# First batch loaded into output tiles, its last tokens for several pairs at once, and feed-forward products moved among the last key tiles

## The chip, the cores and the metric

The kernel runs on one core of one Trainium2 chip. The core has TensorE (PE in the profile, PEld for its weight loads), VectorE (DVE), ScalarE (ACT), GpSimd (POOL) and SyncE (SP), each with a list of its own that it works off in order, and 16 DMA engines. SP and ACT issue transfers on hardware queues (q1, q10), POOL on the software queue (q0), which also converts types. The metric is the device time of one execution in microseconds; lower is better.

## The reference

```python
def _attn_ref(q, k, v, tau):
    q_n = q / (np.linalg.norm(q, axis=-1, keepdims=True) + 1e-06)
    k_n = k / (np.linalg.norm(k, axis=-1, keepdims=True) + 1e-06)
    scores = np.matmul(q_n, k_n.transpose(0, 1, 3, 2)) / tau
    scores = scores - np.max(scores, axis=-1, keepdims=True)
    attn = np.exp(scores)
    attn = attn / (np.sum(attn, axis=-1, keepdims=True) + 1e-09)
    return np.matmul(attn, v)
# x = attention output, (batch, heads, seq, dim) -> (batch * seq, heads * dim)
h = x @ w_in
out = np.maximum(0.01 * h, h) @ w_out
```

q, k and v are (8, 12, 448, 64) in 32-bit floats, tau is 0.1, x is 3584 x 768, w_in 768 x 2048 and w_out 2048 x 768. So: attention on normalised queries and keys, then two dense layers with a leaky ReLU between them.

## The kernel before

**Pairs.** Work on attention goes by pairs of heads, six to a batch, numbered 0 to 47 (called s). A pair's q and k, 448 tokens each, come in three parts: 384 main tokens of q, 384 of k (each token row of 64 numbers, three rows in line to a partition), and the last 64 tokens of both, q's on partitions 0 to 63 and k's on 64 to 127 of one slot. `load_qk` (L126) issues four transfers for a pair: two for the main tokens (192 KB each), two for the last tokens (32 KB each). They go into one of four buffers (`ldp`, L50), and so pair s + 4 can be asked for only when pair s has been normalised.

**Steps of a pair.** `squares` (L193, POOL, for the first pairs also ACT and DVE) squares q and k; `sums` (L208, DVE) adds up the 64 squares of each row, in two parts: q with the last tokens, and k; `roots` (L224, ACT) takes the root as an exponential of half a logarithm; `normalise` (L232, DVE) adds the small constant, inverts, and multiplies into bf16; `transposes` (L281) turns the result on PE and copies it from the accumulator memory with DVE (`qkT`). Then `scores` (L315) multiplies keys by queries in key tiles of 128 tokens on PE, and ACT takes the exponential (L338). Key tile 3 holds the last 64 keys of two pairs, so odd pairs have four tiles and even ones three.

**Quads.** Two pairs make a quad (four heads, called j). `totals` (L356) adds up the exponentials with products with ones and inverts them on ACT; `products` (L366) multiplies by v, once for each half e of the dimensions; `scale` (L375, DVE) multiplies by the inverse into `xT` (L340), the transposed attention output in bf16, one tile for two batches, two buffers (`xtp`, L60). Row block kt = 2 j + e of `xT` belongs to quad j and half e.

**Feed-forward.** Batch c is a chunk of 384 or 512 tokens. `first` (L466) makes one of 16 row blocks of the hidden layer from six products over kt (one accumulator bank), and ACT evicts it through the leaky ReLU (L483); `second` (L489) multiplies by w_out and DVE copies the result (L516). `first` could be split in two parts, kt below a limit and the rest. w_in is loaded in four transfers by POOL (`load_w_in`, L103): even kt and odd kt of the first half of its columns, then of the second half.

**Order.** The whole order is written out by hand up to pair 12; after that a planner spreads feed-forward work over the visits of key tiles. Before the loop over the six pairs of batch 0 (L621 to L677), pair 0 and most of pair 1 are prepared (L548 to L617). The loop runs scores of pair s beside the preparation of pairs s + 1 to s + 3. `fill` (L573) multiplies a constant tile: 22 products ahead of everything, then two or three at the places where it is called. Behind the loop (L688 to L747) feed-forward products of chunk 0 run among the key tiles of batch 1. `hold` (L583) is a copy of one column on POOL, which makes POOL's list wait for a tile before it issues further loads. Accumulator banks are dealt by `banks` (L76): the oldest free one, or a pair of them for a key tile; a bank can be kept under a name.

**Waiting of transfers.** SP's and ACT's transfers use eight completion counters in turn, so a transfer is issued only when the eighth before it has landed. POOL's transfers have eight of their own.

Of the kernel before, what the change touches and what calls it, by code (L numbers as in the profile page):

```python
# [16 lines left out]
def kernel(  # L17
# [108 lines left out]
    def load_qk(s, engs=(nc.sync, nc.sync), rem_engs=None):  # L126
        if s >= NSLOT:
            return
        whole = ldp.tile([128, 14 * D], F32, name="qk_h")
        if s >= OLD:  # L130
            u, which = divmod(s - OLD, 2)
            for w, pair in enumerate(UNITS[u][1]):
                b, h0 = pair // NPAIR, 2 * (pair % NPAIR)
                nc.sync.dma_start(
                    out=whole[64 * w : 64 * w + 64],
                    in_=(q, k)[which][b, h0 : h0 + 2].rearrange("h (p t) d -> (h p) (t d)", t=14),
                )
            raw[s] = whole
            return
        b, h0 = s // NPAIR, 2 * (s % NPAIR)  # L140
        q_h, k_h = halves(whole)
        engs[0].dma_start(out=q_h[:, :, 0:3], in_=main(q, b, h0, 2))
        engs[1].dma_start(out=k_h, in_=main(k, b, h0, 2))
        for i, (x, eng) in enumerate(zip((q, k), rem_engs or engs)):
            eng.dma_start(
                out=q_h[64 * i : 64 * i + 64, :, 3],
                in_=x[b, h0 : h0 + 2, MAIN:S].rearrange("h p d -> p h d"),
            )
        raw[s] = (q_h, k_h)
# [318 lines left out]
    def first(c, m, lo=0, hi=KT):  # L468
        c0, n = chunk_cols(c)
        if c not in hT:  # L470
            hT[c] = htp.tile([128, MT, 512], BF16, name="hT")
        pm = begun.pop((c, m)) if lo else banks(1)
        for kt in range(lo, hi):
            nc.tensor.matmul(  # L474
                out=pm[:, :n],
                lhsT=w_in_sb[:, kt, m * 128 : (m + 1) * 128],
                rhs=xT[c // 2][:, kt, c0 : c0 + n],
                start=(kt == 0), stop=(kt == KT - 1),
            )
        if hi < KT:  # L480
            begun[c, m] = pm
            return
        nc.scalar.activation(out=hT[c][:, m, :n], in_=pm[:, :n], func=AF.Prelu, alpha=0.01)  # L483
# [63 lines left out]

    load_qk(0, (nc.sync, nc.scalar))  # L548
    load_qk(1, (nc.sync, nc.scalar), (nc.sync, nc.sync))
    load_qk(2)  # L550
    load_qk(3)
# [69 lines left out]
    for s in range(NPAIR):  # L621
# [3 lines left out]
        last = s == NPAIR - 1  # L625
        if s == 1:
            roots(2)
        scores(s, (0,))
# [6 lines left out]
        if not last:  # L635
            normalise(s + 1)
            load_qk(s + 5)
# [4 lines left out]
        if last:  # L642
            load_w_out(0)
# [3 lines left out]
        if s == 0:  # L647
            sums(2)
            load_v_rem(0, range(2, 4))
# [5 lines left out]
        elif s != 1:  # L655
            load_w_in(max(s - 1, 0))
# [3 lines left out]
        if not even or s == 0:  # L660
# [15 lines left out]
        if j is not None and not even:  # L676
# [14 lines left out]
    scale(late.pop(), 1)  # L691
    totals(j)
    sums(s)
# [15 lines left out]
    sums(s + 1)  # L709
    feed_groups(0, 1)  # L710
    transposes(s)
    roots(s + 1)
    feed_groups(0, 1)
# [3 lines left out]
    feed_groups(0, 1)  # L717
    scores(s, (0, 1, 2))
    feed_groups(0, 1)
# [218 lines left out]
```

## Time and profile before

| | |
|---|---|
| median of three runs | 421.89 us (420.99 to 422.38) |
| profiled execution, its own time | 421.03 us |
| its span, first to last instruction | 419.2 us |
| PE, ACT, DVE, POOL busy | 98%, 61%, 53%, 28% |
| filler products on PE up to 60 us | 15.59 us, 53 products |
| DMA, mean over the span | 128 GB/s; 207 GB/s in the first 60 us |

In the profile's rows "L329" is a line of the kernel before. A row of the timeline gives the start in microseconds from the span's start, the length, the engine, the line, the operation, the tile written and the tile read, the shapes, how many instructions were merged, and in brackets how long the engine had stood idle and what ended that. A row of the windows gives a stretch, its length, and the busy time and count of each engine. Matmuls overlap, so a busy PE is not PE at its peak; what matters is whether its list has gaps.

### The profile page before, as it was taken

To read this page: it belongs to the slowest core of one execution; us is meant where nothing else is said; L and a number is where in the kernel's file an instruction comes from. 1 tells how busy PE (TensorE), PEld (TensorE's weight loads), DVE (VectorE), ACT (ScalarE), POOL (GpSimd) and SP (SyncE) were. 2 spreads that over 40 slices of the span, in tenths; PEclk is the share of its full clock that TensorE was granted. 3 is DMA by queue.
4 is the path that set the end of the run, shared out by engine and by line. 5 is a ranking of instruction groups with operands and counts; after the bars stand their busy time and mean duration, and the time that the engine had idled before them with its cause. 6 is when DMAs were issued, how large, how long until landed. Compare 5 with 4: busy or idle time off the path is not lost.

```text
span 419.2 us, 11328 instructions
## 1 busy us (share of the span) xinstructions
PE 410.0 (98%) x4797; PEld 211.9 (51%) x4797; DVE 223.0 (53%) x385; ACT 254.4 (61%) x430; POOL 116.6 (28%) x149
## 2 busy tenths in 40 slices
PE   7899999999999999999999999999999999999996
PEld 2334555544455555544455555554445555654563
DVE  6886886874687555864583864464621311210021
ACT  4896877377766686757874778547764364014300
POOL 3877472431433223512430523131210000000000
PEclk9999999999999999999999999999999999999999
DMA  6999999485387932884275592743441100010021
GB/s 164 173 232 231 221 236 225 107 238 113 84 196 224 215 79 57 203 205 115 60 181 160 126 233 74 170 121 89 90 89 52 66 38 3 38 77 0 2 75 75
DMA packets 41906, 53.82 MB, mean 128 GB/s; under 512 B 12544, under 2 KB 32256, under 8 KB 41856
## 3 DMA queue, kind: packets, MB, share of 16 engines
q1 hardware_dynamic: 25680, 40.88, 34.9%
q0 software_dynamic: 15488, 11.80, 19.8%
q8 instruction: 37, 0.61, 0.6%
q10 hardware_dynamic: 688, 0.43, 0.4%
q14 instruction: 13, 0.11, 0.1%
HBM read 45.61 MB, written 11.01 MB: 135 GB/s over the span
## 4 chain that ended last, share of the span: by engine, by line
PE 89%; DMA 3%; DVE 3%; ACT 3%; issue 0%; SPq 0%; DVEq 0%
PE ps L505 35%; PE ps L474 33%; PE ps L425 9%; PE ps L400 7%; PE ps L349 3%; DMA qk_h<-in_q_dram 3%; DVE qn L253 2%; ACT pe L338 1%; PE ps L329 1%; PE ps L576 1%; DMA qk_h<-in_k_dram 1%; PE ps L267 1%; ACT ss L227 0%; ACT hT L483 0%; ACT norms L228 0%
## 5 line engine op out<-in xcount | busy, mean ns | idle before, releaser
L505 PE MATMUL ps<-w_out_sb,hT 128*128 128x384 bf16 x896 | 151.3, 326 | 0.4 <-DVE xT L380 0.4
L474 PE MATMUL ps<-xT,w_in_sb 128*128 128x384 bf16 (+1 forms) x768 | 150.8, 353 | 0.0
L406 ACT ACTIVATE pe<-ps 128x896 bf16<-128x896 f32 x126 | 108.9, 915 | 44.6 <-PE ps L400 44.6
L505 PEld LDWEIGHTS <-hT 128*128 128x128 bf16 x896 | 85.5, 98 | 65.2 <-issue 10.3
L474 PEld LDWEIGHTS <-w_in_sb 128*128 128x128 bf16 x768 | 72.8, 98 | 74.0 <-issue 9.2
L483 ACT ACTIVATE hT<-ps 128x384 bf16<-128x384 f32 (+1 forms) x128 | 67.6, 550 | 54.1 <-PE ps L474 53.6
L516 DVE COPY osb<-ps 128x384 f32<-128x384 f32 (+1 forms) x56 | 30.8, 551 | 101.3 <-PE ps L505 100.3
L199 POOL TENSOR_TENSOR sq<-qk_h 128x896 f32<-128x896 f32 x36 | 60.5, 1681 | 3.3 <-DMA qk_h<-in_k_dram 3.2
L585 POOL CAST seen<-qn 128x1 f32<-128x1 bf16 x46 | 8.9, 193 | 173.7 <-DVE qn L243 168.0
L243 DVE TENSOR_TENSOR qn<-qk_h,r 128x896 bf16<-128x896 f32 x36 | 42.5, 1182 | 1.4 <-DVE r L237 0.2
L338 ACT ACTIVATE pe<-ps 128x896 bf16<-128x896 f32 x42 | 35.9, 915 | 2.4 <-PE ps L329 2.3
L214 DVE TENSOR_REDUCE ss<-sq 128x14 f32<-128x896 f32 x36 | 37.3, 1037 | 0.0
L400 PE MATMUL ps<-qkT 64*32 64x448 bf16 x1008 | 36.5, 353 | 0.0
L236 DVE TENSOR_REDUCE r<-norms 128x14 f32<-128x28 f32 x48 | 8.6, 179 | 49.2 <-ACT norms L228 48.7
L227 ACT ACTIVATE ss<-ss,tiny 128x14 f32<-128x14 f32 x48 | 14.7, 306 | 28.5 <-DVE ss L214 25.6
L450 DVE TENSOR_TENSOR xT<-ps,rb 128x448 bf16<-128x448 f32 x32 | 18.4, 617 | 22.3 <-PE ps L425 21.2
L289 DVE STREAM_TRANSPOSE tt<-qn 128x448 f32<-128x448 f32 x36 | 29.6, 821 | 0.9
L425 PE MATMUL ps<-pe,vq 64*32 64x448 bf16 x1008 | 27.0, 349 | 0.0
L206 POOL TENSOR_TENSOR sq<-qk_h 128x384 f32<-128x384 f32 (+1 forms) x21 | 20.8, 1009 | 14.9 <-DMA qk_h<-in_k_dram 14.9
L400 PEld LDWEIGHTS <-qkT 64*32 64x32 bf16 x1008 | 13.2, 91 | 19.3 <-issue 14.5
L425 PEld LDWEIGHTS <-vq 64*32 64x32 bf16 x1008 | 14.5, 93 | 8.0 <-issue 0.3
L253 DVE TENSOR_TENSOR qn<-qk_h,r 128x512 bf16<-128x512 f32 (+1 forms) x24 | 18.2, 798 | 0.4
(52 smaller groups left out, 215.8 us busy)
## 6 DMA issues: line engine op xcount, KB each, us to landing
qk_h<-in_q_dram SPq DMA_DIRECT2D x36, 224.0 KB, 4.3
qk_h<-in_k_dram SPq DMA_DIRECT2D x36, 224.0 KB, 4.4
out_dram<-osb SPq DMA_DIRECT2D x20, 384.0 KB, 3.0
qkT<-tt SPq DMA_DIRECT2D x72, 56.0 KB, 3.3
qkT<-tt SPq DMA_DIRECT2D x36, 112.0 KB, 3.5
vq<-in_v_dram POOLq DMA_DIRECT2D x16, 224.0 KB, 5.1
w_in_sb<-in_moe_w_in_dram POOLq DMA_DIRECT2D x4, 768.0 KB, 11.1
w_out_sb<-in_moe_w_out_dram POOLq DMA_DIRECT2D x2, 1536.0 KB, 22.6
```

The costliest lines, as they stand in the source:

```text
L199: gp.tensor_tensor(sq, raw[s], raw[s], op=ALU.mult)
L214: nc.vector.tensor_reduce(ss[s], sqs[s].rearrange("p (t d) -> p t d", d=D), axis=AX.X, op=ALU.add)
L243: nc.vector.tensor_tensor(qn[s].rearrange("p m d e -> p m e d"), raw[s].rearrange(f"p ({t[1:-1]} d) -> p m e d", e=n, d=D), r.rearrange(f" ...
L289: nc.vector.transpose(out=to.rearrange(("p g (c m) -> p m g c", "p g (m c) -> p m g c")[which], m=7), in_=qn[s].bitcast(F32).rearrange("p ...
L338: nc.scalar.activation(out=dst, in_=sc[:, :, :S], func=AF.Exp, scale=inv_tau)
L400: nc.tensor.matmul(out=sc[32 * strip : 32 * strip + 32, a, :S], lhsT=x[rows, c0 : c0 + 32], rhs=x[rows, 0:S], start=True, stop=True,)
L406: nc.scalar.activation(out=pq[u, i], in_=sc[:, :, :S], func=AF.Exp, scale=inv_tau)
L425: nc.tensor.matmul(out=po[32 * strip : 32 * strip + 32, w, :S], lhsT=weights, rhs=pq[us[x if two else 0], i][rows, a, :], start=(i == 0), ...
L474: nc.tensor.matmul(out=pm[:, :n], lhsT=w_in_sb[:, kt, m * 128 : (m + 1) * 128], rhs=xT[c // 2][:, kt, c0 : c0 + n], start=(kt == 0), stop= ...
L483: nc.scalar.activation(out=hT[c][:, m, :n], in_=pm[:, :n], func=AF.Prelu, alpha=0.01)
L505: nc.tensor.matmul(out=po2[:, :HALF], lhsT=hT[c][:, m, ts * 128 : (ts + 1) * 128], rhs=w_out_sb[:, m, half * HALF : (half + 1) * HALF], st ...
L516: nc.vector.tensor_copy(out=o[:, half * HALF : half * HALF + cut], in_=po2[:, :cut])
```

## The change

**Loads.** The two `xT` buffers are taken ahead of their use as 32-bit tiles `early`, each for three pairs of batch 0. `load_main` puts a pair's main q and k there; `load_rem` loads the last tokens of one, two or three pairs with one transfer for q and one for k. All six pairs are asked for at the start: main 0, rem 0, main 1, rem 1 and 2, main 2, main 3, rem 3 to 5, main 4, main 5. `load_qk` serves pairs from 6 on; pair 6 is asked for before the loop, pairs 7 to 9 at s = 0, 1 and 2. The first writing into `xT` by `scale` is at s = 3.

**Order before and in the loop.** Pair 0 is normalised ahead of pair 1's sums. POOL holds on pair 0's k, then loads two heads' last tokens of v, then squares pair 1. Pair 2's sums go behind the transposes of pair 1, pair 2's roots behind the first key tile of pair 1. The second w_in transfer goes out at s = 1 instead of s = 2 and there ahead of the v load of s = 2. At s = 5 the second half of quad 1 is scaled and the sums of pairs 6 and 7 are taken.

**Feed-forward.** `first` takes any list of kt and goes on where it stopped, keeping its bank. At s = 5 the two fillers behind key tile 2 and key tile 3 are replaced: row blocks 0 and 1 do kt 0 and 2, then kt 1. Behind the loop they do kt 3, row blocks 2 and 3 do kt 0 to 3, and after the transposes of pair 6 all four do kt 4 and 5. Pair 6's roots and normalise are put ahead of the totals and scalings of quad 2.

```diff
+    early = [xtp.tile([128, 6, 7, D], F32, name="xT") for _ in range(2)]
+
+    def load_rem(pairs, engs=(nc.sync, nc.sync)):
+        lo, hi = 2 * (pairs[0] % 3), 2 * (pairs[-1] % 3) + 2
+        part = early[pairs[0] // 3][:, lo:hi, 3]
+        for i, (x, eng) in enumerate(zip((q, k), engs)):
+            eng.dma_start(
+                out=part[64 * i : 64 * i + 64],
+                in_=x[0, 2 * pairs[0] : 2 * pairs[-1] + 2, MAIN:S].rearrange("h p d -> p h d"),
+            )
+
+    def load_main(s, engs=(nc.sync, nc.sync)):
+        whole = early[s // 3][:, 2 * (s % 3) : 2 * (s % 3) + 2]
+        q_h, k_h = raw[s] = whole[:, :, 0:4], whole[:, :, 4:7]
+        engs[0].dma_start(out=q_h[:, :, 0:3], in_=main(q, 0, 2 * s, 2))
+        engs[1].dma_start(out=k_h, in_=main(k, 0, 2 * s, 2))
...
-    def first(c, m, lo=0, hi=KT):
+    def first(c, m, kts=range(KT)):
...
-        pm = begun.pop((c, m)) if lo else banks(1)
-        for kt in range(lo, hi):
+        if (c, m) in begun:
+            pm, done = begun.pop((c, m))
+        else:
+            pm, done = banks(1, (c, m, "begun") if len(kts) < KT else None), 0
+        for i, kt in enumerate(kts):
...
-    load_qk(0, (nc.sync, nc.scalar))
-    load_qk(1, (nc.sync, nc.scalar), (nc.sync, nc.sync))
-    load_qk(2)
-    load_qk(3)
+    load_main(0, (nc.sync, nc.scalar))
+    load_rem((0,), (nc.sync, nc.scalar))
+    load_main(1, (nc.sync, nc.scalar))
+    load_rem((1, 2))
+    load_main(2)
+    load_main(3)
+    load_rem((3, 4, 5))
+    load_main(4)
+    load_main(5)
...
     roots(0)
+    hold(raw[0][1][:, 0, 0, 0:1])
+    load_v_rem(0, range(2))
     squares(1, (nc.scalar, gp))
+    normalise(0)
     sums(1, (1,))
-    normalise(0)
-    load_qk(4)
-    load_v_rem(0, range(2))
+    load_qk(6)
     hold(qn[0][:, 6, 0, 0:1])
     squares(2)
     load_v(0)
+    load_v_rem(0, (2,))
...
+        scores(s, (0,))
         if s == 1:
             roots(2)
-        scores(s, (0,))
...
             normalise(s + 1)
-            load_qk(s + 5)
+        if s < 3:
+            load_qk(s + 7)
...
         if last:
+            scale(j, 1)
+            sums(NPAIR)
+            sums(NPAIR + 1)
             load_w_out(0)
...
         if s == 0:
-            sums(2)
-            load_v_rem(0, range(2, 4))
+            load_v_rem(0, (3,))
...
-        elif s != 1:
-            load_w_in(max(s - 1, 0))
+        elif s < 2:
+            load_w_in(s)
+        elif s > 2:
+            load_w_in(s - 1)
...
-        if not even or s == 0:
+        if last:
+            for m in range(2):
+                first(0, m, (0, 2))
+        elif not even or s == 0:
             fill(2)
...
             transposes(s + 1)
+        if s == 0:
+            sums(2)
...
-        if not even or s == 0:
+        if last:
+            for m in range(2):
+                first(0, m, (1,))
+        elif not even or s == 0:
             fill(2)
...
-    scale(late.pop(), 1)
+    roots(s)
     totals(j)
-    sums(s)
+    normalise(s)
...
     for m in range(2):
-        first(0, m, 0, KT - 2)
+        first(0, m, (3,))
+    for m in range(2, 4):
+        first(0, m, range(KT - 2))
     for e in range(2):
         scale(j, e)
-    roots(s)
-    for m in range(2):
-        first(0, m, KT - 2)
-    work[0] = work[0][2:]
-    normalise(s)
+    roots(s + 1)
     load_qk(s + 4)
     hold(qn[s][:, 6, 0, 0:1])
     squares(s + 3)
-    sums(s + 1)
-    feed_groups(0, 1)
     transposes(s)
-    roots(s + 1)
-    feed_groups(0, 1)
+    for m in range(4):
+        first(0, m, range(KT - 2, KT))
+    work[0] = work[0][4:]
     normalise(s + 1)
     load_qk(s + 5)
     sums(s + 2)
-    feed_groups(0, 1)
     scores(s, (0, 1, 2))
-    feed_groups(0, 1)
+    feed_groups(0, 2)
     transposes(s + 1)
```

More of the change, by code (lines that the diff above doesn't have):

```diff
@@ L141, in load_qk @@
         q_h, k_h = halves(whole)
[L142 to L145, printed above, removed]
+        nc.sync.dma_start(out=q_h[:, :, 0:3], in_=main(q, b, h0, 2))
+        nc.sync.dma_start(out=k_h, in_=main(k, b, h0, 2))
+        for i, x in enumerate((q, k)):
+            nc.sync.dma_start(
                 out=q_h[64 * i : 64 * i + 64, :, 3],
@@ L675 @@
             roots(n)
-        if j is not None and not even:
+        if j is not None and not even and not last:
             late.append(j)
```

10 lines of the change are left out of this document (6 added, 4 removed).

## The prediction

> **What bounds the kernel now.** I read the page first, then the windows, then the timeline of the first 56 us, where all edits lie.
>
> ```profile
> PE 410.0 (98%) x4797; PEld 211.9 (51%) x4797; DVE 223.0 (53%) x385; ACT 254.4 (61%) x430; POOL 116.6 (28%) x149
> PEclk9999999999999999999999999999999999999999
> PE 89%; DMA 3%; DVE 3%; ACT 3%; issue 0%; SPq 0%; DVEq 0%
> ```
>
> PE is busy 98%, its clock was granted in full throughout, and the chain that ended last is 89% PE. But PE is also busy with filler, so the windows decide (stretch and length, then busy us and count of PE, PEld, DVE, ACT, POOL; the second row counts only the filler line L576, on PE and PEld).
>
> ```profile
> 10.75:34.60 23.85, 21.53 (x217) 8.13 (x216) 19.42 (x39) 21.64 (x33) 19.20 (x27) 1.00 1.10 212
> 10.35:36.49 26.14, 8.51 (x29) 1.71 (x28) 1.00 1.10 213
> 100.00:160.00 60.00, 60.00 (x837) 32.02 (x835) 38.78 (x61) 44.62 (x76) 19.15 (x23) 1.00 0.65 158
> ```
>
> Three stages follow. Up to 10.75 us the first pair's load and its norms stand in line. From there to 34.60 the six pairs of batch 0 run and ACT is busy 21.64 of 23.85 us, so its idle 2.2 us is all a better order can win there; PE has 8.51 us of filler beside it. From 36.49, where feed-forward products begin, PE has no idle time (60.00 of 60.00): what is left for PE at that point fixes the end. A saving is therefore either an earlier 36.49, or feed-forward products done before it, or a stall of PE behind it.
>
> **The change, part by part.** Instructions keep their lengths; only their places and waits move. Rows are start, length, engine, line, operation, and in brackets the idle time before it and what ended it.
>
> ```profile
> 6.40 0.83 POOL L206 TENSOR_TENSOR sq<-qk_h 128x384 f32<-128x384 f32 x1 [5.09 <-DMA qk_h<-in_k_dram]
> 6.59 0.22 ACT L228 ACTIVATE norms<-ss 128x14 f32<-128x14 f32 x1
> 7.26 0.63 ACT L204 ACTIVATE sq<-qk_h 128x512 f32<-128x512 f32 x1 [0.45 <-DMA qk_h<-in_k_dram]
> 7.26 0.55 DVE L220 TENSOR_REDUCE ss<-sq 128x6 f32<-128x384 f32 x1 [1.04 <-POOL sq L206]
> 7.73 0.17 DVE L236 TENSOR_REDUCE r<-norms 128x14 f32<-128x28 f32 x1
> 9.29 0.68 DVE L220 TENSOR_REDUCE ss<-sq 128x8 f32<-128x512 f32 x1
> 9.88 0.35 DVE L615 COPY qkT<-ps 128x384 bf16<-128x384 bf16 x1
> 10.35 0.55 PE L329 MATMUL ps<-qkT 64*128 64x448 bf16 x4
> ```
>
> *Start.* Pair 0's roots end at 6.81, yet its normalise begins at 7.73, because DVE first waits for pair 1's squares. The change puts normalise first: 6.84, 0.89 earlier. Normalise takes 1.56 to the next instruction (7.73 to 9.29), then come both sums of pair 1 (0.47 and 0.59 from row to row), so the copy starts at 6.84 + 1.56 + 0.47 + 0.59 = 9.46 instead of 9.88. Scores of pair 0 start 0.42 earlier, at 9.93. This needs ACT's square of pair 1 by 8.87, so its last tokens by 8.2; they are now one transfer for pairs 1 and 2, twice the packets. Bounds for its landing: as before, 7.26; and 8.1, if it takes the 4.4 from issue that pair 1's 192 KB of k took to the first row (issued at 2.03; the new transfer at about 3.7). Both are in time: no cost. Without that cover each further us is one us of the end. The new hold on POOL (pair 0's k) and the two v loads stand ahead of pair 1's squares; they end by 6.1 against that square's 6.40, so they are free. SP issues six transfers fewer by the end of pair 5, and pairs 4 to 6 no longer wait for a buffer; each transfer still waits for the eighth before it.
>
> ```profile
> 12.64 1.13 DVE L220 TENSOR_REDUCE ss<-sq 128x8 f32<-128x512 f32 x2
> 13.69 0.61 DVE L308 COPY qkT<-ps 128x896 bf16<-128x896 bf16 x1
> 14.15 0.22 ACT L228 ACTIVATE norms<-ss 128x14 f32<-128x14 f32 x1
> 14.36 0.55 PE L329 MATMUL ps<-qkT 64*128 64x448 bf16 x4 [0.81 <-ACT norms L228]
> 14.77 1.73 ACT L338 ACTIVATE pe<-ps 128x896 bf16<-128x896 f32 x2 [0.40 <-PE ps L329]
> 15.29 1.16 DVE L253 TENSOR_TENSOR qn<-qk_h,r 128x512 bf16<-128x512 f32 x2
> 16.37 0.55 DVE L220 TENSOR_REDUCE ss<-sq 128x6 f32<-128x384 f32 x1
> 17.17 0.32 ACT L227 ACTIVATE ss<-ss,tiny 128x14 f32<-128x14 f32 x1
> 17.64 3.46 ACT L338 ACTIVATE pe<-ps 128x896 bf16<-128x896 f32 x4
> ```
>
> *Pairs 0 and 1.* Pair 2's sums (1.13) now stand behind pair 1's copy: that copy starts at 12.64 instead of 13.69, the scores of pair 1 at 13.31 instead of 14.36, their first exponential at 13.72 instead of 14.77. That 1.05 is not kept. Pair 2's sums run to 14.37; its roots, now behind that exponential, to 15.05 (before 14.37); its normalise starts at 15.56 (before 15.29), pair 3's sums end at 17.2 (before 16.92), pair 3's roots start at 17.23 (before 17.17), and the exponential behind them, the first of a run of four, at 17.70 instead of 17.64. From there ACT had no gap to 23.4. I take +0.1 for pairs 0 to 4, between -1.0 (all kept) and +0.5 (pair 2's squares collide, below).
>
> *Pair 5.* Two fillers of two (row at 33.56) go; six products of chunk 0 take their place.
>
> ```profile
> 31.99 2.61 ACT L338 ACTIVATE pe<-ps 128x896 bf16<-128x896 f32 x3 [0.25 <-PE ps L329]
> 33.56 0.61 PE L576 MATMUL ps<-pe 128*128 128x512 bf16 x2
> 34.10 0.75 PE L349 MATMUL ps<-pe,ones 128*32 128x448 bf16 x12
> 36.28 1.16 DVE L380 TENSOR_TENSOR xT<-ps,rb 128x448 bf16<-128x448 f32 x2 [2.89 <-ACT rb L361]
> 36.49 3.10 PE L474 MATMUL ps<-xT,w_in_sb 128*128 128x384 bf16 x18
> 39.93 2.11 PE L474 MATMUL ps<-xT,w_in_sb 128*128 128x384 bf16 x12
> ```
>
> A product is (3.10 - 2.11) / 6 = 0.165. Four and two take 0.66 and 0.33, the fillers that they replace 0.61 each: no longer. ACT ends that stage (exponentials to 34.60, on which the totals' last part waits), so its end does not move; six products leave what follows: -6 x 0.165 = -0.99. The last key tile's scores come about 0.1 later behind four products: +0.1. The sums and roots of pair 6 now precede the last totals on ACT; they fill its wait of 0.49 there. Pair 6's normalise precedes the two scalings, which then end at 38.0 instead of 37.4; ten products (1.65) and the transposes hide that, and without them 0.6 would show.
>
> *Behind 36.49.* Pairs 6 to 11 are prepared beside the products. Their normalises are 1.16 alone, but longer beside POOL's squares, which came late because a load came late.
>
> ```profile
> 26.85 2.00 DVE L253 TENSOR_TENSOR qn<-qk_h,r 128x512 bf16<-128x512 f32 x2
> 27.10 2.44 POOL L206 TENSOR_TENSOR sq<-qk_h 128x512 f32<-128x512 f32 x2 [2.50 <-DMA qk_h<-in_k_dram]
> 45.23 1.82 POOL L206 TENSOR_TENSOR sq<-qk_h 128x512 f32<-128x512 f32 x2 [2.17 <-DMA qk_h<-in_k_dram]
> 46.34 1.74 DVE L253 TENSOR_TENSOR qn<-qk_h,r 128x512 bf16<-128x512 f32 x2
> PEld L267 <- DVE qn L253: 1.2, 5, 0.3
> PE ps L505 <- DVE xT L380: 0.4, 1, 0.4
> ```
>
> The last two rows are waits between 44 and 66 us: 1.6 us in which PE lacked a normalised pair or a scaled chunk. With pairs 6 to 9 loaded ahead (pair 9 is issued at 18 to 20 instead of 28.9) and two pairs' sums done early, a normalise loses the 0.6 to 0.8 of a collision, more than any wait (0.2 to 0.4). But PE also comes about 0.8 earlier. Bounds: 0 and -1.6; I take -0.7, three of the five waits and part of the sixth.
>
> *One rule against it.* Before, the squares of pair 2 and the normalise of pair 1 overlapped and the latter took 1.64; after, they touch at 10.66 if pair 2 lands by 8.8. The Trainium skill, page "SBUF — State Buffer", section "Who interferes with whom", has DVE and GpSimd exclude each other on a shared port for a whole instruction. By that rule, with pair 2 landing as late as before, the normalise would wait up to 1.0, and the sum would be half as good (-0.7); by the row it costs 0.5 and is inside my bound.
>
> *Sum.* +0.1 - 0.99 + 0.1 - 0.7 = -1.5 us. The profiled execution took 421.03 (span 419.2): 419.5 for it. The median of the three runs is 421.89, 0.86 above; so 420.4 for a median, -0.36%. What a measurement of this kernel tells from no change is about 0.3%, 1.27 us.
>
> **The rivals.**
>
> ```profile
> 22.37 0.80 POOL L160 DMA_DIRECT2D v_b<-in_v_dram  x1
> 23.16 0.75 POOL L105 DMA_DIRECT2D w_in_sb<-in_moe_w_in_dram  x1
> w_in_sb<-in_moe_w_in_dram POOLq DMA_DIRECT2D x4, 768.0 KB, 11.1
> q0 software_dynamic: 952, 1.01, 74.4%
> q1 hardware_dynamic: 1767, 1.00, 44.5%
> ```
>
> *Slower: weights late.* The last two of the six products need the odd rows of the first weight, at 33.4. Its load was issued at 23.16, and a load lands 11.1 after its issue; now it goes at 19.7, behind v of pair group 1, so it lands at 30.8. But three more pairs (3 x 448 KB = 1.34 MB) ask before it. The last two rows are packets, MB and share of each queue between 26 and 34 us: together 2.0 MB in 8 us. If all of it went ahead, the load would land 5.4 later, at 36.2; PE would stand 2.8 with the totals behind it, and v of group 2, now queued behind this load, would be late too. Sum +2.8 - 0.99 + 0.2 = +2.0: 423.0, as a median 423.9. It decides from a landing at 35.5. Against it: the rows show both queues moving at once. The Trainium skill, page "DMA: Bandwidth & Descriptors", section "Queues, rings and completion order", has each DMA engine take turns between rings by packet; by that rule the weight's larger packets get the larger share and it lands by about 32, an estimate, with no wait. Chance 0.16.
>
> *No change.* The waits behind 36.49 stay, since ACT's evictions and exponentials still set the roots of pair 8: -0.8, 420.2, median 421.1. For it: the waits are small and each has two causes. Chance 0.29.
>
> *More.* Pair 2's roots find DVE sooner than I reckoned and 1.0 of pairs 0 and 1 is kept: -2.5, median 419.4. Against it: the chain of DVE rows above is complete and has little slack. Chance 0.12.
>
> **How the numbers follow.** My forecast has 0.43. Faster by over 0.3%: 0.43 + 0.12 = 0.55; within: 0.29; slower: 0.16. The range runs from 418.9 (the larger gain and 0.5 of scatter) to 422.3 (0.4 above the median before); the weight stall beyond it is left out. The forecast's own range is 419.7 to 421.0.
>
> **What would show it.** Right: first scores near 9.9 and pair 1's near 13.3; the run of four exponentials near 17.7; filler x48 instead of x52; six products between 32 and 34; the start of the ten products near 36.6; fewer waits of PE for qn. Wrong: PEld waiting at a product before 34.5 (weights late); the run of four later than 18.2 (collision); PE idle behind 36.6 as before.

## The result and the profile after

| | before | changed |
|---|---|---|
| median | 421.96 us (420.92 to 422.91, 16 runs) | 420.03 us (419.61 to 421.29, 16 runs) |
| profiled execution (span) | 421.03 us (419.2) | 419.61 us (417.8) |

The ratio is 0.9958, with a 95% interval of 0.9947 to 0.9969: 1.9 us faster. The prediction was 420.4, with 0.55 on faster; the time lies in its own range and 0.4 us below its centre.

The page of the changed kernel first: busy time by engine, the granted clock, the share of the chain that ended last by engine.

```profile
PE 409.2 (98%) x4793; PEld 212.1 (51%) x4793; DVE 219.8 (53%) x385; ACT 253.7 (61%) x430; POOL 114.8 (27%) x150
PEclk9999999999999999999999999999999999999999
PE 96%; DVE 2%; ACT 2%; issue 0%; DVEq 0%
```

PE was on 89% of that chain before and transfers on 3%; now PE has 96% and transfers do not appear. The windows (stretch, length, then busy us and count of PE, PEld, DVE, ACT, POOL) say much the same of batch 0: ACT is nearly as full as before (idle 2.87 of 24.14 us, before 2.21 of 23.85; the stage starts 0.34 earlier and ends where it did), and PE has no gap behind.

```profile
10.41:34.55 24.14, 21.55 (x215) 8.25 (x217) 19.52 (x41) 21.27 (x33) 20.28 (x29) 1.00 1.17 230
100.00:160.00 60.00, 60.00 (x839) 32.31 (x838) 38.74 (x61) 44.81 (x78) 18.85 (x22) 1.00 0.65 154
```

The timeline of the changed kernel, at the places that the prediction named (L223 and L216 are squares, L270 the normalise, L346 scores, L355 the exponential, L494 feed-forward products, L397 the scaling; pair 2's squares at 8.80, pair 1's normalise at 10.85, pair 12's squares at 56.80, pair 11's normalise at 57.84).

```profile
8.80 1.82 POOL L223 TENSOR_TENSOR sq<-xT 128x512 f32<-128x512 f32 x2
10.00 0.55 PE L346 MATMUL ps<-qkT 64*128 64x448 bf16 x4
10.85 1.16 DVE L270 TENSOR_TENSOR qn<-xT,r 128x512 bf16<-128x512 f32 x2
13.39 0.55 PE L346 MATMUL ps<-qkT 64*128 64x448 bf16 x4 [0.29 <-DVE qkT L325]
17.79 3.32 ACT L355 ACTIVATE pe<-ps 128x896 bf16<-128x896 f32 x4
32.75 0.82 PE L494 MATMUL ps<-xT,w_in_sb 128*128 128x384 bf16 x4
33.82 0.50 PE L494 MATMUL ps<-xT,w_in_sb 128*128 128x384 bf16 x2
33.94 0.92 ACT L355 ACTIVATE pe<-ps 128x896 bf16<-128x896 f32 x1 [0.16 <-PE ps L346]
35.82 1.16 DVE L270 TENSOR_TENSOR qn<-qk_h,r 128x512 bf16<-128x512 f32 x2
36.72 1.80 PE L494 MATMUL ps<-xT,w_in_sb 128*128 128x384 bf16 x10
36.90 1.15 DVE L397 TENSOR_TENSOR xT<-ps,rb 128x448 bf16<-128x448 f32 x2
56.80 1.69 POOL L216 TENSOR_TENSOR sq<-qk_h 128x896 f32<-128x896 f32 x1
57.84 1.67 DVE L270 TENSOR_TENSOR qn<-qk_h,r 128x512 bf16<-128x512 f32 x2
```

The six products stand at 32.75 and 33.82 with no wait ahead of them, where before there was filler, and the ten that follow start at 36.72. Every normalise from pair 1 to pair 10 takes its undisturbed 1.16; only that of pair 11 takes 1.67, beside a square. Of the 1.6 us in which PE waited for normalised pairs and scaled chunks between 44 and 66 us, this row of the waits (us in total, times, longest) is left; no wait for qn is.

```profile
PE ps L527 <- DVE xT L397: 0.5, 1, 0.5
```

Laid side by side, the changed trace is 0.03 us later than before at the exponentials of 32 us. From about 54 us its exponentials and evictions are 1.7 to 1.9 us earlier, and from 75 us to the last eviction 1.8. So nothing is won in the loop over batch 0 itself. The products behind it start 0.23 later (36.72 against 36.49), but six of them, 0.99 us, are already done: 0.76 won. The other 1.03 is won behind that point. The end of the last store gives 0.4 of this back in these two profiled executions (span 1.4 shorter).

### The profile page after: what moved, and what is told of

Read it like the earlier page. It is cut to its first block, busy times and chain, and to the rows that moved or that the text cites. A ratio compares the mean times of both kernels' runs of the same rounds, so it can differ in the third digit from the quotient of the medians.

```text
span 417.8 us, 11304 instructions
## 1 busy us (share of the span) xinstructions
PE 409.2 (98%) x4793; PEld 212.1 (51%) x4793; DVE 219.8 (53%) x385; ACT 253.7 (61%) x430; POOL 114.8 (27%) x150
## 4 chain that ended last, share of the span: by engine, by line
PE 96%; DVE 2%; ACT 2%; issue 0%; DVEq 0%
PE ps L527 36%; PE ps L494 35%; PE ps L442 9%; PE ps L417 7%; PE ps L366 3%; PE ps L603 3%; PE ps L346 2%; PE ps L284 1%; ACT pe L355 1%; DVE qkT L325 0%; DVE qn L270 0%; DVE ss L231 0%; DVE osb L538 0%; ACT ss L244 0%; ACT norms L245 0%
## 5 line engine op out<-in xcount | busy, mean ns | idle before, releaser
L494 PE MATMUL ps<-xT,w_in_sb 128*128 128x384 bf16 (+1 forms) x768 | 151.1, 353 | 0.0
L494 PEld LDWEIGHTS <-w_in_sb 128*128 128x128 bf16 x768 | 72.7, 98 | 74.1 <-issue 9.7
L216 POOL TENSOR_TENSOR sq<-qk_h 128x896 f32<-128x896 f32 x36 | 60.4, 1679 | 3.8 <-DMA qk_h<-in_k_dram 3.8
L355 ACT ACTIVATE pe<-ps 128x896 bf16<-128x896 f32 x42 | 36.0, 919 | 2.9 <-PE ps L346 2.8
L417 PE MATMUL ps<-qkT 64*32 64x448 bf16 x1008 | 36.5, 353 | 0.0
L244 ACT ACTIVATE ss<-ss,tiny 128x14 f32<-128x14 f32 x48 | 14.7, 307 | 26.6 <-DVE ss L231 25.7
L603 PE MATMUL ps<-pe 128*128 128x512 bf16 x49 | 15.5, 443 | 1.6 <-DVE pe L586 1.6
L346 PE MATMUL ps<-qkT 64*64 64x448 bf16 (+1 forms) x132 | 12.8, 360 | 2.5 <-ACT pe L355 1.6
```

The lines of the kernel that those rows point to most:

```text
L216: gp.tensor_tensor(sq, raw[s], raw[s], op=ALU.mult)
L355: nc.scalar.activation(out=dst, in_=sc[:, :, :S], func=AF.Exp, scale=inv_tau)
L417: nc.tensor.matmul(out=sc[32 * strip : 32 * strip + 32, a, :S], lhsT=x[rows, c0 : c0 + 32], rhs=x[rows, 0:S], start=True, stop=True,)
L494: nc.tensor.matmul(out=pm[:, :n], lhsT=w_in_sb[:, kt, m * 128 : (m + 1) * 128], rhs=xT[c // 2][:, kt, c0 : c0 + n], start=(done + i == 0), ...
```

## The experiments

All are edits of the changed kernel, but one of the kernel before; "us lost" is the difference of medians to 420.03 unless a trace is named. Each has its own interval against the kernel before. The changed kernel was not run again beside them, and its profiled execution is the fastest of its sixteen, 0.42 under their median, so that a difference between two traces can be larger than that of the medians.

**The six products.** Fillers back at s = 5, products behind the loop:

```diff
-        if last:
-            for m in range(2):
-                first(0, m, (0, 2))
-        elif not even or s == 0:
+        if not even or s == 0:
             fill(2)
...
-        first(0, m, (3,))
+        first(0, m, range(KT - 2))
```

(and likewise for kt 1 behind key tile 3).

> The changed kernel with the two fillers back at s = 5 and the six products behind the loop again; all else as changed. Theory (six products are worth their own length because PE has no gap behind them): 0.99 us of the gain goes, so about 421.0, ratio to the kernel before 0.998, and every eviction from 66 us on stands 0.8 instead of 1.8 us earlier than before. Rival (the gain is one of loads and norms, the products only fill time that ACT or DVE sets): within 0.3 us of the changed kernel, ratio 0.996.

Measured: 420.77, ratio 0.9976 (0.9967 to 0.9984): 0.74 lost. In its trace the products behind the loop are sixteen:

```profile
36.63 2.77 PE L494 MATMUL ps<-xT,w_in_sb 128*128 128x384 bf16 x16
```

They end near 39.4 where the ten of the changed kernel end at 38.52, and later events are 0.82 us late up to about 82 us (1.19 from 89 us on). The term of 0.99 for the six products is confirmed in kind, and in size to within 0.25.

**The loads of batch 0 as before**, with order and products as changed:

```diff
-    load_main(0, (nc.sync, nc.scalar))
-    load_rem((0,), (nc.sync, nc.scalar))
-    load_main(1, (nc.sync, nc.scalar))
-    load_rem((1, 2))
...
+    load_qk(0, (nc.sync, nc.scalar))
+    load_qk(1, (nc.sync, nc.scalar), (nc.sync, nc.sync))
+    load_qk(2)
+    load_qk(3)
...
-        if s < 3:
-            load_qk(s + 7)
+            load_qk(s + 5)
```

> The changed kernel with the loads of batch 0 as before (four buffers, pair s + 5 asked for when pair s + 1 is normalised, last tokens for each pair alone); order and products as changed. Theory (early loads remove the collisions of POOL's squares with the normalises, worth 0.8 together with the early sums): 0.4 to 0.8 us of the gain goes, ratio 0.9975, and PE waits for qn again behind 44 us (about 1 us, against none in the changed kernel). Rival (early loads are hidden anyway and order does it): ratio stays at 0.996, no waits for qn.

Measured: 422.40, ratio 1.0010 (1.0000 to 1.0021): 2.4 lost, three times what was expected. The waits between 36 and 66 us in its trace:

```profile
POOL sq L222 <- DMA qk_h<-in_k_dram: 4.3, 3, 2.1
PEld L283 <- DVE qn L269: 2.3, 5, 0.7
POOL v_b L176 <- DMA w_out_sb<-in_moe_w_out_dram: 2.0, 1, 2.0
PE ps L526 <- DMA w_out_sb<-in_moe_w_out_dram: 0.6, 1, 0.6
```

Up to 45 us this trace is only 0.28 late. Then the squares of pairs wait for their loads, PE waits for the normalises behind them, and w_out is late too. The trace is 1.64 late at 57 us and 2.84 late from 66 us on: the last 1.2 come where the load of v, held by w_out, puts pair 12's squares on pair 11's normalise (below, "The weights a step ahead"). With the new order and the old loads everything gained is lost again.

**The early sums.** Sums of pairs 6 and 7, their roots and pair 6's normalise in their old places:

```diff
         if last:
             scale(j, 1)
-            sums(NPAIR)
-            sums(NPAIR + 1)
             load_w_out(0)
...
-    roots(s)
     totals(j)
-    normalise(s)
+    sums(s)
...
-    roots(s + 1)
+    roots(s)
+    normalise(s)
     load_qk(s + 4)
     hold(qn[s][:, 6, 0, 0:1])
     squares(s + 3)
+    sums(s + 1)
     transposes(s)
+    roots(s + 1)
```

> The changed kernel with the sums of pairs 6 and 7, the roots of both and the normalise of pair 6 back in their old places behind the totals and scalings of quad 2; loads and products as changed. Theory (PE reaches the transposes of pair 6 after ten products, 1.65 us, and then needs a normalised pair, which the old order gives 2 us later): PE waits 0.5 to 1.5 at those transposes, ratio 0.997 to 0.999. Rival (loads alone gave the 0.8 us): within 0.2 us of the changed kernel, ratio 0.996.

Measured: 421.64, ratio 0.9992 (0.9982 to 1.0001): 1.6 lost. From its timeline and its waits (36 to 66 us):

```profile
38.12 1.16 DVE L270 TENSOR_TENSOR qn<-qk_h,r 128x512 bf16<-128x512 f32 x2
49.81 2.27 POOL L223 TENSOR_TENSOR sq<-qk_h 128x512 f32<-128x512 f32 x2 [1.80 <-DMA qk_h<-in_k_dram]
50.39 2.10 DVE L270 TENSOR_TENSOR qn<-qk_h,r 128x512 bf16<-128x512 f32 x2
PEld L284 <- DVE qn L270: 1.3, 4, 0.7
```

Pair 6 is normalised 2.30 us later (38.12 against 35.82), the next pairs some 1.5, and PE waits for them again. Pair 10 is asked for 2.3 us later, and its squares wait 1.80 for it. So with the rest in place the early sums are worth more than the 0.7 that the prediction put behind 36.5 us, and more than the 1.03 measured there. Part of it is cover: eighteen products stood ahead of pair 6's transposes before (to 39.59), ten do now, and in this run they end at 38.58 while pair 6's normalise ends at 39.28.

**The loads alone.** The kernel before with only the new loads:

```diff
-    load_qk(0, (nc.sync, nc.scalar))
-    load_qk(1, (nc.sync, nc.scalar), (nc.sync, nc.sync))
-    load_qk(2)
-    load_qk(3)
+    load_main(0, (nc.sync, nc.scalar))
+    load_rem((0,), (nc.sync, nc.scalar))
+    load_main(1, (nc.sync, nc.scalar))
+    load_rem((1, 2))
...
-            load_qk(s + 5)
+        if s < 3:
+            load_qk(s + 7)
```

> The kernel before with one part of the change alone: the loads (batch 0 into the early tiles, last tokens for several pairs at once, pairs 6 to 9 asked for at the places of the changed kernel); order of the work and feed-forward as before. Theory of parts that need each other: taking the loads out of the changed kernel lost 2.4 us, taking the early sums out 1.6 us, the six products 0.75, more together than the 1.9 gained; so alone the loads give less than 2.4: their pairs land early, but the sums and roots of pairs 6 and 7 are still late, and PE still waits for these: -0.3 to -0.9 us, 421.1 to 421.7. Rival of parts that add up: alone they give their whole 2.4 us, about 419.6. Rival of no use alone: within 0.3 us of 421.96.

Measured: 421.17, ratio 0.9979 (0.9970 to 0.9989): 0.8 gained against the kernel before. Removed from the changed kernel the loads cost 2.4, added to the kernel before they bring 0.8. So the parts do not add up; they need each other. What is still in the way with loads alone:

```profile
38.04 1.16 DVE L270 TENSOR_TENSOR qn<-qk_h,r 128x512 bf16<-128x512 f32 x2
49.45 2.27 POOL L223 TENSOR_TENSOR sq<-qk_h 128x512 f32<-128x512 f32 x2 [1.61 <-DMA qk_h<-in_k_dram]
49.76 2.37 DVE L270 TENSOR_TENSOR qn<-qk_h,r 128x512 bf16<-128x512 f32 x2
```

Pair 6 is as late as in the last experiment, pair 10 can be asked for only when pair 6 is normalised, its squares wait 1.61 for it and then lie over pair 9's normalise, which takes 2.37.

**The last tokens of pairs 1 to 5 each alone** (six more transfers of 32 KB), then of pairs 3 to 5 only (four more):

```diff
-    load_rem((1, 2))
+    load_rem((1,))
     load_main(2)
+    load_rem((2,))
     load_main(3)
-    load_rem((3, 4, 5))
+    load_rem((3,))
     load_main(4)
+    load_rem((4,))
     load_main(5)
+    load_rem((5,))
```

> The changed kernel with the last tokens of pairs 1 to 5 loaded for each pair alone: six transfers more on SP, the same bytes and packets. Theory (their number is hidden): within 0.3 us of the changed kernel, ratio 0.996; the scores of pair 0 start at 10.0 as now. Rival (each small transfer costs its 0.6 us of issue and a turn in the window of eight, and pairs 2 to 6 come later by up to 3 us): pair 2's squares wait on POOL, the run of four exponentials starts 0.3 to 1.0 later than 17.8, ratio 0.997 to 0.998.

> The changed kernel with the last tokens of pairs 3, 4 and 5 each loaded alone (four more transfers), those of pairs 1 and 2 together as changed. In e3_rem_single, with all of pairs 1 to 5 alone, 1.66 us were lost: 0.47 in the loop (pair 2's squares late and colliding) and the rest behind 45 us (pairs 9 and 10 late). Theory that each transfer waits for the eighth before it: four more transfers push the asking for pairs 6 to 9 back, pair 9 lands 5 us or more later (41 or later in place of 36), squares of pair 9 or 10 wait, and 0.5 to 1.2 us are lost behind 45 us, with the loop unchanged: 420.5 to 421.2. Rival: what e3 lost behind 45 us came from the loop's own 0.5 us later w_out and loads of v, and pair 2 alone is the cause: 420.0 to 420.2 here.

Measured: 421.69, ratio 1.0001 (0.9986 to 1.0016), for pairs 1 to 5; 420.37, ratio 0.9969 (0.9956 to 0.9982), for pairs 3 to 5. So 1.7 and 0.3 us are lost. That six more transfers would be hidden was my theory for the first, and it fell. Its timeline:

```profile
10.05 2.27 POOL L223 TENSOR_TENSOR sq<-xT 128x512 f32<-128x512 f32 x2 [1.26 <-DMA xT<-in_k_dram]
10.70 2.03 DVE L270 TENSOR_TENSOR qn<-xT,r 128x512 bf16<-128x512 f32 x2
46.06 2.24 POOL L223 TENSOR_TENSOR sq<-qk_h 128x512 f32<-128x512 f32 x2 [3.08 <-DMA qk_h<-in_k_dram]
51.03 1.82 POOL L223 TENSOR_TENSOR sq<-qk_h 128x512 f32<-128x512 f32 x2 [2.60 <-DMA qk_h<-in_k_dram]
```

Two things are seen. Pair 2 is late, its squares start at 10.05 in place of 8.80 and lie over pair 1's normalise, which takes 2.03 in place of 1.16 (0.47 lost in the loop). And pair 9's last part landed at 45.9 and pair 10's at 50.9, against 36.0 and 46.4 in the changed kernel. The run with only pairs 3 to 5 apart:

```profile
40.69 2.02 POOL L223 TENSOR_TENSOR sq<-qk_h 128x512 f32<-128x512 f32 x2 [3.27 <-DMA qk_h<-in_k_dram]
48.17 2.27 POOL L223 TENSOR_TENSOR sq<-qk_h 128x512 f32<-128x512 f32 x2 [1.81 <-DMA qk_h<-in_k_dram]
58.02 2.80 DVE L270 TENSOR_TENSOR qn<-qk_h,r 128x512 bf16<-128x512 f32 x2
58.10 1.69 POOL L216 TENSOR_TENSOR sq<-qk_h 128x896 f32<-128x896 f32 x1
```

The loop is unchanged here (-0.11), and pair 9 lands at 40.5: later, as the theory that a transfer waits for the eighth before it has it. By itself that costs nothing, for at 50 us the trace is still 0.11 ahead. But pair 10's squares then come 1.65 late and lie over pair 9's normalise (2.11), at 58 us those of pair 12 lie over pair 11's (2.80), and behind that the trace is 0.95 late. Of the 3.21 by which the trace of the first run ends up late, 1.0 comes at the same place. The median of the second run lies between the two expectations, and its interval overlaps the changed kernel's, so that its 0.3 is not clear of the noise; the times of the first run scatter over 2.8 us. By the medians most of the 1.7 hangs on the transfer for pairs 1 and 2 together; that the waiting for the eighth before alone does it is not shown.

**Pairs 8 and 9 asked for later** (at s = 3 and 4 in place of 1 and 2), and **the odd rows of w_in later** (s = 2 in place of 1):

```diff
-        if s < 3:
-            load_qk(s + 7)
+        if s in (0, 3, 4):
+            load_qk(7 if s == 0 else s + 5)
```

```diff
-        elif s < 2:
-            load_w_in(s)
-        elif s > 2:
-            load_w_in(s - 1)
+        elif s != 1:
+            load_w_in(max(s - 1, 0))
```

> The changed kernel with pairs 8 and 9 asked for at s = 3 and s = 4 instead of s = 1 and s = 2; nothing else moved. Theory (it is the late landing of these two pairs behind the weight loads that makes POOL's squares late and collide): POOL waits for a load at the squares of pairs 8 and 9 again, normalises of 1.7 to 2.0 return, and 0.4 to 0.8 us of the gain goes, ratio 0.997 to 0.998. Rival (the early sums and roots of pairs 6 and 7 alone give PE and DVE their lead): within 0.2 us of the changed kernel.

> The changed kernel with the second weight transfer back at s = 2, behind the v load there. In the kernel before, a weight load landed 11 us after its issue; issued near 23.2 it lands near 34.2. Theory (the fifth and sixth product need it at 33.8, and PE's list stands until it is there): PE waits 0.3 to 0.8 at the fifth product, the totals behind it start as much later, and the end moves by the same, ratio 0.997 to 0.998. Rival (the load is in time, since early loads of q and k leave the engines free by then): no wait at that product, ratio 0.996.

Measured: 420.28, ratio 0.9964 (0.9952 to 0.9976), and 420.19, ratio 0.9952 (0.9938 to 0.9967). Neither can be told from the changed kernel.

The first edit does not do what it was meant to do. Nothing else stands on SP's list at these steps, so its transfers keep their order, and each goes out when the eighth before it has landed. The first transfer of pair 9, in the changed kernel and in this run:

```profile
20.48 0.59 SPq L159 DMA_DIRECT2D qk_h<-in_q_dram  x1
21.34 0.59 SPq L159 DMA_DIRECT2D qk_h<-in_q_dram  x1
```

Pair 9's transfers go out from 20.48 to 24.43 and have landed by 35.99 in the changed kernel; here they go out from 21.34 to 23.55 and have landed by 36.96. Whether the time at which pairs 8 and 9 are asked for counts is therefore not tested by this run.

The second edit does what it says. The odd rows go out at 23.36 in place of 19.70 and land at 34.07 in place of 30.98, and the last two of the six products wait for them:

```profile
34.12 0.50 PE L494 MATMUL ps<-xT,w_in_sb 128*128 128x384 bf16 x2 [0.15 <-DMA w_in_sb<-in_moe_w_in_dram]
```

Later events are 0.2 to 0.3 us late, 0.1 of it from before the products. So the theory is right that the products wait, but the wait is 0.15 and not 0.3 to 0.8. A whole step later the prediction's slower rival, w_in late, has just begun.

**The order at the start.** Pair 0's normalise behind pair 1's sums of k again:

```diff
     squares(1, (nc.scalar, gp))
-    normalise(0)
     sums(1, (1,))
+    normalise(0)
```

> The changed kernel with pair 0's normalise behind pair 1's sums of k again, as before. Theory of the prediction: scores of pair 0 start 0.3 to 0.4 us later (10.35 in place of 10.00) and pair 1's scores too, but VectorE's row behind it sets pairs 0 to 4, and pair 1's chain has no spare time either: +0.3 us or a little more at the run of four exponentials (18.1 in place of 17.79), and +0.3 at the end, 420.4. Rival: the gap behind pair 0's exponentials takes it up, nothing is seen at the run of four and the time stays at 420.0.

Measured: 420.69, ratio 0.9975 (0.9961 to 0.9988): 0.66 lost, where 0.3 were expected.

```profile
7.21 0.83 POOL L223 TENSOR_TENSOR sq<-xT 128x384 f32<-128x384 f32 x1 [1.14 <-DMA xT<-in_k_dram]
8.07 0.55 DVE L237 TENSOR_REDUCE ss<-sq 128x6 f32<-128x384 f32 x1 [1.70 <-POOL sq L223]
11.16 0.55 PE L346 MATMUL ps<-qkT 64*128 64x448 bf16 x4
```

DVE stands 1.70 us for pair 1's squares with pair 0's normalise behind; scores of pair 0 start at 11.16, and the run of four exponentials 1.16 later than in the changed kernel. The gap behind pair 0's exponentials does not take it up, as the rival had it. In this execution pair 1's k came 0.46 later than in the changed kernel's (7.21 against 6.75), so the trace shows more than the medians.

**Keeping the 1.0 us of pair 1.** Pair 2's sums in DVE's gaps ahead of pair 1's copy, and its roots in ACT's gap:

```diff
         copy(out=dst[:, lo:hi], in_=tp[:, lo:hi])
+    sums(2, (0,))
     fill(3)
...
-        scores(s, (0,))
         if s == 1:
             roots(2)
+        scores(s, (0,))
...
-        if not last:
-            transposes(s + 1)
         if s == 0:
-            sums(2)
+            sums(2, (1,))
+        if not last:
+            transposes(s + 1)
```

> A version meant to keep the 1.0 us that pairs 0 and 1 win and lose again: pair 2's sums are put in two gaps of DVE (its first part behind pair 0's copy, its second ahead of pair 1's copy), and its roots in ACT's gap ahead of pair 1's first exponential. Theory (the roots of pair 2 behind that exponential are what delays the normalise of pair 2, the sums and roots of pair 3 and the run of four exponentials): pair 1's scores start 0.1 to 0.3 later than 13.4, the run of four starts at 16.8 to 17.2 instead of 17.8, the end moves by as much, 0.6 to 1.0 us under the changed kernel, ratio 0.993 to 0.995. Rival (behind that run PE or the loads set the time of pairs 2 to 5): the run starts earlier and the products behind the loop do not, ratio 0.996.

Measured: 420.39, ratio 0.9958 (0.9941 to 0.9975): nothing gained. The run of four exponentials starts 0.78 earlier; of this 0.45 is left from 22 us on and 0.24 from 40 us to 57 us. Then:

```profile
57.96 2.29 PE L527 MATMUL ps<-w_out_sb,hT 128*128 128x384 bf16 x13 [1.16 <-DMA w_out_sb<-in_moe_w_out_dram]
58.45 0.82 POOL L177 DMA_DIRECT2D v_b<-in_v_dram  x1 [2.69 <-DMA w_out_sb<-in_moe_w_out_dram]
```

The next limit is the landing of w_out's first half, at 57.9 us in this execution; behind it the trace is 0.98 late. It is not a fixed time: in the changed kernel's trace the same load went out 0.45 later (30.95 against 30.50) and had landed at 54.27. The rival that a later limit would take the gain is right for this run.

**The weights a step ahead** of that:

```diff
         if last:
             scale(j, 1)
             sums(NPAIR)
             sums(NPAIR + 1)
-            load_w_out(0)
...
-        elif s < 2:
-            load_w_in(s)
-        elif s > 2:
-            load_w_in(s - 1)
+        elif s < 4:
+            load_w_in(s)
+        else:
+            load_w_out(0)
```

> The changed kernel with pair 2's sums in VectorE's gaps and its roots in ScalarE's gap (as in e7_gap_sums2), and with the third and fourth w_in transfers and the first half of w_out each issued one step of the loop earlier (s = 2, 3, 4 in place of 3, 4, 5). Theory: what took the 0.8 us of e7 back was the landing of w_out near 57.9 us; issued some 3 us earlier (before: 30.50 in e7) it lands before 57, PE does not wait at line L527's first product, and the 0.5 to 0.8 us stays to the end: about 419.3, a ratio of 0.994 to the kernel before. Rival: the DMA engines are full between 20 and 45 us, so the weights that go earlier only push the q and k of pairs 7 to 9 back, and the squares of one of these wait: same as e7 or up to 1 us longer, 420.4 to 421.5.

Measured: 420.38, ratio 0.9965 (0.9952 to 0.9977). The edit moved w_out's first half from 30.50 only to 29.55, and it landed at 56.08. The trace is 0.6 us ahead of the changed kernel's up to pair 11's normalise and 0.3 behind it afterwards. GpSimd's rows, and the normalise:

```profile
29.55 1.21 POOL L111 DMA_DIRECT2D w_out_sb<-in_moe_w_out_dram  x1
...
32.55 0.81 POOL L177 DMA_DIRECT2D v_b<-in_v_dram  x1
33.36 2.49 POOL L185 DMA_DIRECT2D v_rem<-in_v_dram  x4
...
47.68 0.82 POOL L177 DMA_DIRECT2D v_b<-in_v_dram  x1
48.49 1.17 POOL L111 DMA_DIRECT2D w_out_sb<-in_moe_w_out_dram  x1
...
56.62 0.82 POOL L177 DMA_DIRECT2D v_b<-in_v_dram  x1 [1.21 <-PE ps L346]
57.24 2.94 DVE L270 TENSOR_TENSOR qn<-qk_h,r 128x512 bf16<-128x512 f32 x2
57.46 1.69 POOL L216 TENSOR_TENSOR sq<-qk_h 128x896 f32<-128x896 f32 x1
```

The load of v at 56.62 stood 1.21 us. Counted back (1 + 1 + 4 + 1 + 1) the eighth transfer before it is w_out's first half. The squares of pair 12 stood behind it on GpSimd's list, and so fell on pair 11's normalise: 2.94 in place of 1.16. The scores that the row names as the releaser cannot be it, since in the changed kernel the same load went out at 55.95, ahead of those scores (56.28).

The other traces bear this out. In seven of the fourteen this load goes out 0.53 to 0.54 us after w_out's first half has landed (here 56.62 after 56.08; in the kernel before 58.04 after 57.51); in the other seven w_out had landed 1.4 us or more ahead of it. Where the load is held and the squares of pair 12 then meet pair 11's normalise, five traces, the normalise takes 1.97 to 3.23; where it is not held, 1.67 to 1.74.

**That load behind the squares**, as a test of this reading:

```diff
-    load_v(s // 2 + 2)
     load_qk(s + 7)
     squares(s + 6)
+    load_v(s // 2 + 2)
```

> e8_gap_w_ahead with one load moved: v of quad 4, on GpSimd's list, goes behind the squares of pairs 11 and 12 instead of between them. In e8 that load waited 1.21 us at 56.62; counted back on GpSimd's queue the eighth transfer before it is the first half of w_out, which PE too waited for at 56.3; the squares of pair 12 stood behind it, started at 57.46 and lay over the normalise of pair 11 (57.24), which took 2.94 in place of 1.16. Theory: with the load behind them the squares start near 55.4 and end by 57.1, the normalise takes 1.16 to 1.2, PE finds its transposes on time, the 0.6 us that e8 had in hand up to 57.8 stays, and every later event is 0.5 to 0.6 us earlier than in the changed kernel: span 417.2 to 417.4, median 419.3 to 419.6, ratio 0.994. Rival: the wait has another owner (the key tile's scores that the trace names, or pair 12's own load): the squares start after 57 all the same, or v comes late and PE waits for it at quad 4: 420.3 or more.

Measured: 419.64, ratio 0.9941 (0.9928 to 0.9955), over five runs from 419.03 to 420.68. The profiled one is the slowest of the five:

```profile
55.81 1.67 POOL L216 TENSOR_TENSOR sq<-qk_h 128x896 f32<-128x896 f32 x1
57.59 2.77 PE L527 MATMUL ps<-w_out_sb,hT 128*128 128x384 bf16 x16 [0.70 <-DMA w_out_sb<-in_moe_w_out_dram]
57.69 1.16 DVE L270 TENSOR_TENSOR qn<-qk_h,r 128x512 bf16<-128x512 f32 x2
58.08 0.82 POOL L177 DMA_DIRECT2D v_b<-in_v_dram  x1 [0.60 <-DMA w_out_sb<-in_moe_w_out_dram]
```

The collision is gone: the squares start at 55.81, the normalise takes 1.16, and the load now names w_out as what it waited for. So the reading is right. But in this execution w_out itself landed at 57.6 although it was issued at 29.6, and PE stood 0.70 for it. Of the 0.5 us that this trace was ahead of the changed kernel's up to 38 us, 0.2 were left from 40 us on; it is 0.6 behind after that wait, and 0.5 more from 84 us, where PE waited 0.4 for a transfer of transposed queries and keys. The median is below the changed kernel's, but the two intervals against the kernel before overlap, and the two were not run side by side: a small further gain is likely, not shown.

## Why the prediction was right, point by point

**What bounds the kernel.** The three stages held: ACT sets batch 0 (21.27 of 24.14 us busy after), and behind it PE has no idle time (60.00 of 60.00), so that only products moved ahead and PE's own waits could count.

**The start, -0.42.** Scores of pair 0 started at 10.00 (predicted 9.93, before 10.35). The step was right. The 0.07 that is missing is pair 0's normalise, which took 1.31 in place of 1.16 beside the end of pair 1's square. Taken back alone the step costs 0.66, because pair 1's k lands later than before and the old order waits for it: GpSimd's square of it starts at 6.75 in the changed kernel and at 7.21 in the run with the old order, where it stood at 6.40. GpSimd's new hold and the v loads are not what delays that square, for they had been issued by 6.17 and it then waited 0.59 for the k. Why the k lands later is open.

**Pairs 0 and 1, the 1.05 not kept.** Scores of pair 1 at 13.39 (predicted 13.31), the run of four at 17.79 (predicted 17.70). Shift at 32 us: +0.03 for the +0.1 taken. The rival "more" named this place. A better order there did win 0.78, of which 0.24 was left when w_out's landing took it back; the prediction did not see that.

**The six products, -0.99 and +0.1.** They took fillers' places (49 filler products after, 53 before; the prediction wrote 48 and 52) and delayed the last key tile's exponential by 0.2, and the products behind the loop by 0.23; taken back, 0.74.

**Behind 36.49, -0.7.** This is the mis-sized term: it measured -1.03 between the traces. The waits of PE went from 1.6 to 0.5. Two of the reasons were off. The transfers saved were counted at nothing, as "six transfers fewer"; six put back cost 1.7. And pair 9 goes out at 20.48 to 24.43, not at 18 to 20, because its transfers wait for the eighth before; whether its early asking counts by itself is not shown.

What makes the stage faster is the joint effect: pairs 6 and 7 normalised early free the buffers for pairs 10 and 11, and pairs loaded early leave the queue free for them. In the changed kernel pair 10 is asked for at 37.06, has landed by 46.36, and its squares do not wait. Without the early sums it is asked for at 39.37 (39.28 with the loads alone), lands by 49.65 (49.29), and its squares wait 1.80 (1.61). With the old loads it is asked for at 37.58, nearly as early, but pair 9's transfers have then not landed (the last at 45.08); pair 10 lands by 50.04 and its squares wait 2.03.

**The rule weighed.** In the changed kernel the squares of pair 2 (8.80 to 10.62) and pair 1's normalise (10.85) do not touch, so the rule cost nothing there, as the prediction's condition (pair 2 landed by 8.8) had it. Where runs made a square start 0.1 to 0.2 us behind a normalise, the Trainium skill's page "SBUF — State Buffer", section "Who interferes with whom" (DVE and GpSimd exclude each other for a whole instruction on a shared port), agrees with the rows: beside a square of 1.69 the normalise took 2.94 and 2.80, that is 1.78 and 1.64 over its 1.16, nearly the length of the square. In both the normalise had started first, by 0.22 and 0.08, and it was still the one that lost; why is open. With the two overlapping by 1.62 in the run with last tokens apart, it lost only 0.87 and the squares 0.45 over their 1.82; there the loss was shared.

**The rivals.** "Weights late" did not come: the odd rows landed at 30.98 (the prediction had 30.8 without delay, about 32 with both queues taking turns, and 36.2 at worst), 2.8 us before the products that read them. With the load one step later, at 34.07, they waited 0.15. "No change" did not come: the waits for qn went. "More" did not come.

**Sum.** -1.5 was predicted for the profiled execution, -1.42 measured (421.03 to 419.61). That these lie so close is partly luck: up to the last eviction the terms measured +0.03 + 0.2 - 0.99 - 1.03 = -1.79, and the last store gave 0.4 back, which the prediction did not have. Between the medians it is -1.93, since the new median lies only 0.42 above its profiled execution, where the prediction added the 0.86 of before; this part is scatter.

## What to carry to other kernels

A reorder of loads and a reorder of work that depends on them are worth little apart and more together (here 0.8 for the loads alone, 2.4 when they are taken out of the whole), so price them as one step and ask which buffer each frees. On a queue whose transfers wait for the eighth before them, small transfers and one big slow one both set when the next is issued, and the compute that stands behind that issue on the same engine moves with it; count back eight at each late issue. When an early gain vanishes later, look for the one landing that did not come earlier with it. And moving a load in the program moves nothing when its queue has nothing else to do: see in the trace whether the issue moved before reading the time.

## What the runs showed of the hardware that was not expected

The price of a VectorE normalise beside a GpSimd square depends on how they meet: 1.16 alone, 1.67 when the square has 0.65 us left, 2.03 when both take parts in turn, 2.80 to 3.23 when one square of 1.69 starts 0.1 to 1.1 us after it (four traces). So 0.6 us of lead turned into 0.3 us of loss by moving one start by some tenths.

The first half of w_out (1536 KB in the profile's list) was issued between 29.55 and 36.11 us in the fourteen traces and landed between 51.94 and 59.21. The time of issue tells little of the landing: 29.62 led to 57.55, and 31.12 to 51.94. In all fourteen it landed 11.1 to 14.7 us after the transfer ahead of it on GpSimd's queue, the fourth part of w_in, had landed. The third part of w_in is alike: it went out at 26.39 in the changed kernel and had landed at 37.40; sent at 22.69, with the weights a step ahead, it had landed at 37.47. So on this queue asking 3.7 us earlier brought nothing. What sets the 11.1 to 14.7 us was not measured.

The times of the changed kernel fall in two groups, twelve of 419.61 to 420.31 and four of 421.00 to 421.29. The collision at 57 us, which cost 0.8 to 1.2 us in four traces and hangs on the landing of w_out, would explain them; no trace of one of the four was seen, so this stays open.
